# A scaled absolute value in the weights' conversion, a gap ahead of the gate tiles, ten sums on TensorE in place of twelve, and a new table of due times

## The chip, the cores and the metric

The kernel runs on one NeuronCore of a Trainium2 chip. The metric is the device time of one execution in microseconds (us). Before the change it is 534.67 us, the median of three runs (533.86 to 534.92). One further execution was taken with the profiler; everything that is said of single instructions comes from it.

## What is computed

Sliding-window attention over 8 batches, 8 heads, 576 positions of 64 elements, and behind it a feed-forward block with a gate:

```
scores = q @ k.T / 8, masked: heads 0-3 see the last 32 positions, heads 4-7 every 4th of the last 128
attn = softmax(scores); x = (attn @ v), heads side by side   # 8 x 576 x 512
h = relu(x @ w_in)                                           # 8 x 576 x 1024
conv = 3-tap convolution of h along the positions, per channel
out = (h * sigmoid(conv)) @ w_out                            # 8 x 576 x 512
```

The weights `w_in`, `w_out` and the taps arrive as 64-bit floats; everything else is 32-bit. The kernel reads each 64-bit weight as two 32-bit words and makes float32 numbers of them itself. Matrix products of `x` with `w_in` and of the gated `h` with `w_out` are made in a faster 32-bit format that keeps fewer bits, so each operand is kept as a high and a low part, and three products (high x high, high x low, low x high) are added.

## The kernel before

**Work.** The eight heads of a batch are handled in pairs, four pairs `p` a batch `b`, so 32 pairs; a pair is numbered `4 * b + p` here. Pairs with `p` 0 and 1 have the plain window (tensors `qk_p`, `v_p`), those with 2 and 3 the dilated one (`qk_d`, `v_d`). `attention` makes for each pair: two loads (L266 query and key, L268 value), the scores on TensorE (L294), a softmax on VectorE and ScalarE, a transpose on VectorE (L341), the product with the values on TensorE (L352), and the split of the result into a high part (`x..a`, ScalarE, L404) and a low part (`x..b`, VectorE, L407).

For the pairs in `EASED` the mask is added on TensorE (L281 puts it into the bank ahead of the scores), VectorE finds the maximum in the bank (L307, L309), and ScalarE makes nine exponentials with their sums (L318). For the others VectorE adds the mask (L323, L326), finds the maximum, subtracts it and sums (L328, L330, L334), and ScalarE makes one exponential of the whole tile (L332). Scores and products of the values stand in one set of banks, `att`, of which there is a single one: the scores of one pair, or the products of the values of one pair, hold it until the last reader is done. The scores of the pairs in `EARLY` stand in three other banks (`mm`, `mm`, `nn`).

`expert` makes for each batch the first product (L432: 16 groups of 12 matmuls with 288 columns, 1536 in all; even groups take columns 0 to 287 of `x`, odd groups 288 to 575), relu (L439), the taps (L450, L444), the sigmoid (L455), the gating (L457), the split into `g..a` and `g..b` (L460, L462), and the second product (L474: 24 matmuls with 512 columns for each 128 rows, 864 in all; `g` is the stationary operand, `wo` the one that moves). Results are copied out of the bank (L485) and stored (L488).

**Weights.** `weights` converts one block of 128 x 512 weights; there are 8 of `w_in`, 8 of `w_out`, and the small one of the taps. ScalarE takes the absolute value of the high words (L506); VectorE limits it from below (L508), shifts it (L510), puts sign and top bits back (L512), takes out the power of two (L515) and scales the low words (L517). For the blocks in `SUMMED` (counted 0 to 7 in `w_in`, 8 to 15 in `w_out`) ScalarE rounds to the high part (L523), TensorE sums the rest from three products (L526 to L528: with the identity, and twice with its negative), and ScalarE copies the low part out of the bank (L531). For the others VectorE adds (L533), ScalarE rounds (L538), VectorE subtracts (L539).

**Order.** No engine's order is written out. Each step is given to `Planner` with a cost, a due time, what it follows and which buffers it takes. The planner takes for each engine what can start first and, within `WINDOW`, what is due first. Due times come from the tables `DUE`, `PAIR`, `WI`, `WO`, `EXTRA`, and `SHIFT`, which moves single steps by their number. On the chip every engine works through its list strictly in that order. All transfers are issued from SyncE's list (SP), which waits in order too.

**Places.** The tiles of `const` lie one behind the other in each partition. By the program's addresses the tiles `wi` and `wo` begin 96 bytes past a multiple of 256 bytes, `x` and `g` 224 bytes past one; columns 288 on of `x` begin 96 bytes past one.

Of the kernel before, what the change touches and what calls it, by code (L numbers as in the profile page):

```python
# [8 lines left out]
F32 = mybir.dt.float32  # L9
# [4 lines left out]
AF = mybir.ActivationFunctionType  # L14
ALU = mybir.AluOpType
AX = mybir.AxisListType

B, H, S, D = 8, 8, 576, 64
# [18 lines left out]
    0: (983.85, 960.03, 1598.27, 67.97, 620.34, -923.1),  # L37
    1: (-938.0, 1528.76, 586.65, 116.27, 1083.92, -668.08),
    2: (652.26, -238.47, 216.19, -384.77, 936.91, 1546.14),
    3: (-577.95, 582.66, 797.36, 1055.27, 486.95, 100.42),  # L40
    4: (165.44, 367.0, 655.84, 266.33, 368.22, -114.96),
    5: (-900.42, 829.96, 667.81, -687.56, 659.06, -189.44),
    6: (8.73, -696.85, -879.8, 781.86, 1623.94, -212.82),
    7: (119.25, -702.72, 113.74, 318.1, 576.55, 91.32),
}
PAIR = {
    0: (-798.09, -868.3, -581.71, -552.22),
    1: (-227.57, -1850.41, -372.89, -477.4),
    2: (-1.4, 42.43, -131.58, 110.75),
    3: (118.94, 167.04, 351.66, 219.64),  # L50
    4: (363.37, 135.93, -216.08, 368.31),
    5: (629.07, 791.29, 654.94, 920.11),
    6: (1389.29, 1178.72, 41.99, 1049.45),
    7: (1485.93, 1267.62, 1424.81, 1415.74),
}
WI = (298.37, -257.47, 97.32, -1419.26, 580.38, -902.1, -1795.13, -709.05)
WO = (614.53, -200.78, 56.88, 710.98, 973.01, 906.23, 1376.69, 1432.54)
EXTRA = (-811.84, -256.46, -1474.23, 929.81, -481.76, 986.25, -195.54, -589.31, -887.09, -1471.19, -474.02, 685.32, 2263.81, 148.88, 1433.56, 2268.02, 97.62, -454.37, 119.84, 1449.84, 204.84, 29.37, 164.77, 787.77, 157.69, 1023.44, -135.34, -139.5, -1509.68, 1495.81, -788.12, -964.17, 519.88, -547.13, 138.9)

SHIFT = {  # L60
# [14 lines left out]
EASED = range(8)  # L75
EARLY = (1, 2, 3)
SUMMED = range(12)
# [21 lines left out]
class Planner:  # L99

    LATENCY = {"DVE": 0.05, "ACT": 0.05, "SP": 2.3, "POOL": 0.1, "E": 0.2, "S": 0.33, "T": 0.35, "V": 0.2}
# [5 lines left out]
              "TE": 0.11, "TV": 0.2, "TS": 0.2}  # L107
# [80 lines left out]
def attn_moe(ctx: ExitStack, tc: tile.TileContext, qk_p, qk_d, v_p, v_d, w_in, w_out, conv, mask, out):  # L188
    nc = tc.nc
# [25 lines left out]
    slots("x", NX, [128, S], F32R, 2)  # L215
    slots("g", NF, [128, S + REST], F32R, 2)
# [38 lines left out]
    def attention(b, p):  # L255
# [10 lines left out]
        lq = plan.add("SP", n * 0.00147, due - EXTRA[32], lambda: nc.sync.dma_start(  # L266
            out=qk.t[:, :n], in_=(qk_p, qk_d)[kind][b, p % 2]), uses=[qk])
        lv = plan.add("SP", 1.13, due - EXTRA[33], lambda: nc.sync.dma_start(  # L268
# [147 lines left out]
    def expert(b, ready, wired, wored, conved):  # L416
# [52 lines left out]
        for u, (first_col, rows) in enumerate(blocks):  # L469
# [7 lines left out]
            for k in range(NF):  # L477
                last = plan.add("PE", 0.68, out_due + by_block * u + by_step * k, lambda a=(first_col, ps, k): second(*a),
                                [last, wored[k], gates[k]], [ps, g[k]], "E")
                if b % 2 == 0:  # L480
                    read.setdefault((b, k), []).append(last)
# [10 lines left out]
    def weights(src, n, due, dst=None, pair=None, summed=False):  # L492
# [7 lines left out]
        last = plan.add("SP", 0.1 + 1.4 * f, due - EXTRA[34], lambda: nc.sync.dma_start(  # L500
            out=both(), in_=src.bitcast(I32).rearrange("p (n t) -> p n t", t=2)), uses=[raw])

        def step(cost, uses, run):
            return plan.add("DVE", 0.16 + cost * f, due + EXTRA[21], run, [last], uses)

        last = plan.add("ACT", 0.16 + 0.5 * f, due + EXTRA[20], lambda: nc.scalar.activation(  # L506
            out=words(u), in_=high().bitcast(F32), func=AF.Abs), [last], [raw, u])
        last = step(0.265, [u], lambda: nc.vector.tensor_scalar(  # L508
            out=words(u), in0=words(u), scalar1=2.0 ** -15, scalar2=None, op0=ALU.max))
        last = step(0.265, [u], lambda: nc.vector.tensor_scalar(  # L510
            out=ints(u), in0=ints(u), scalar1=3, scalar2=0x3fffffff, op0=ALU.logical_shift_left, op1=ALU.bitwise_and))
        last = step(0.53, [raw, u, t], lambda: nc.vector.scalar_tensor_tensor(  # L512
            out=ints(t), in0=high(), scalar=-0x40000000, in1=ints(u), op0=ALU.bitwise_and, op1=ALU.bitwise_or))
# [144 lines left out]
```

## Time and profile before

| | |
|---|---|
| time, median of 3 runs | 534.67 us (533.86 to 534.92) |
| the profiled execution's own time | 531.44 us |
| its span, first to last instruction | 529.7 us |
| mean granted TensorE clock | 0.993 |
| last matmul begins | 525.52 us after the span's start |

A row of the page's first part gives an engine's busy time, its share of the span and its instructions; the second part cuts the span in 40 slices of 13.2 us and gives a tenth-digit for each. A row of the timeline gives start and duration in us, engine, line and operation; a row of the windows gives, for a stretch, each engine's busy time and instructions, then TensorE's granted clock, the share of the DMA engines and GB/s. PE is TensorE, PEld its loads of the stationary operand, DVE VectorE, ACT ScalarE.

### The profile page before, as it was taken

The numbers are of one execution on the slowest core, as the hardware profiler recorded it, in microseconds if no ns is written. First come the engines' busy times: TensorE is split into PE (matmuls) and PEld (weight loads), VectorE is DVE, ScalarE is ACT, GpSimd is POOL, SyncE is SP. The second block draws the span as 40 slices with busy tenths as digits, with TensorE's granted clock in tenths as the row PEclk, the third lists the DMA queues.
The fourth block names the chain that finished last, engine by engine and source line by source line (L and its number), as shares of the span: only waits on it lengthen the run. The fifth ranks groups of instructions, "written<-read, shape, count | busy, mean of one in ns | idle before, by whom it ended". The sixth has DMA issues, their size and how long they took to land.

```text
span 529.7 us, 17200 instructions
## 1 busy us (share of the span) xinstructions
PE 507.5 (96%) x7668; PEld 440.5 (83%) x7668; DVE 396.1 (75%) x686; ACT 307.3 (58%) x661; POOL 1.4 (0%) x26
## 2 busy tenths in 40 slices
PE   4679999999999999999999999999999999999997
PEld 3458889898777799889999878998799978998885
DVE  5879999999987799888877887688556677475400
ACT  6776887756732279537776534666655534583410
POOL 1000000000000000000000000000000000000000
PEclk9979999999999999999999999999999999999999
DMA  8886663001344540250120444133211020010011
GB/s 296 312 292 221 186 208 111 1 1 41 111 160 150 179 153 0 75 187 2 29 73 1 152 145 131 51 101 104 79 42 41 0 88 24 1 41 22 31 49 59
DMA packets 17274, 52.33 MB, mean 99 GB/s; under 512 B 2096, under 2 KB 2480, under 8 KB 17200
## 3 DMA queue, kind: packets, MB, share of 16 engines
q1 hardware_dynamic: 17200, 51.23, 29.2%
q8 instruction: 60, 0.98, 0.8%
q14 instruction: 14, 0.11, 0.1%
HBM read 41.79 MB, written 9.44 MB: 97 GB/s over the span
## 4 chain that ended last, share of the span: by engine, by line
PE 93%; DVE 3%; issue 2%; ACT 1%; DMA 1%; SPq 0%; ACTq 0%; DVEq 0%
PE banks L474 39%; PE banks L432 39%; PE banks L352 7%; PE banks L294 6%; PE banks L526 1%; DMA qk<-in_qk_p_dram 1%; DVE s L339 1%; ACT s L318 1%; PE banks L281 0%; DVE m L307 0%; DVE r L517 0%; DVE pt L341 0%; DVE w L512 0%; PE banks L527 0%; PE banks L528 0%
## 5 line engine op out<-in xcount | busy, mean ns | idle before, releaser
L444 DVE SCALAR_TENSOR_TENSOR u<-u,conv_sb,u 128x576 f32<-128x576 f32 x128 | 104.2, 818 | 22.4 <-ACT u L450 20.6
L439 ACT ACTIVATE u<-banks 128x288 f32<-128x288 f32 x128 | 50.6, 410 | 50.9 <-PE banks L432 50.4
L457 DVE TENSOR_TENSOR u<-u,u 128x576 f32<-128x576 f32 x64 | 48.2, 758 | 22.7 <-ACT u L455 21.8
L455 ACT ACTIVATE u<-u 128x576 f32<-128x576 f32 x64 | 43.6, 686 | 31.0 <-DVE u L444 30.7
L485 ACT COPY u<-banks 128x512 f32<-128x512 f32 (+1 forms) x37 | 21.1, 574 | 61.4 <-PE banks L474 56.2
L432 PE MATMUL banks<-x5a,wi 128*128 128x288 f32 x192 | 53.5, 295 | 0.0
L450 ACT ACTIVATE u<-u,conv_sb 128x576 f32<-128x576 f32 x64 | 49.8, 778 | 1.5
L352 PEld LDWEIGHTS banks<-pt,v 32*64 32x64 f32 x2752 | 35.4, 133 | 15.8 <-issue 7.9
L294 PEld LDWEIGHTS banks<-qk 64*32 64x32 f32 x2432 | 30.0, 110 | 18.6 <-issue 9.7
L432 PE MATMUL banks<-x2a,wi 128*128 128x288 f32 x160 | 45.3, 298 | 0.0
L352 PE MATMUL banks<-pt,v 32*64 32x64 f32 (+2 forms) x2752 | 39.2, 229 | 6.2 <-issue 1.9
L294 PE MATMUL banks<-qk 64*32 64x64 f32 x2432 | 36.0, 234 | 9.3 <-DMA qk<-in_qk_p_dram 4.7
L432 PE MATMUL banks<-x0a,wi 128*128 128x288 f32 x160 | 44.9, 295 | 0.0
L432 PE MATMUL banks<-x6a,wi 128*128 128x288 f32 x160 | 44.7, 294 | 0.0
L432 PE MATMUL banks<-x4a,wi 128*128 128x288 f32 x160 | 44.5, 296 | 0.0
L432 PEld LDWEIGHTS banks<-x5a,wi 128*128 128x128 f32 x192 | 35.9, 187 | 0.4
L432 PEld LDWEIGHTS banks<-x6a,wi 128*128 128x128 f32 x160 | 30.0, 188 | 0.5
L432 PEld LDWEIGHTS banks<-x0a,wi 128*128 128x128 f32 x160 | 30.0, 188 | 0.4
L432 PEld LDWEIGHTS banks<-x2a,wi 128*128 128x128 f32 x160 | 30.0, 188 | 0.4
L432 PEld LDWEIGHTS banks<-x4a,wi 128*128 128x128 f32 x160 | 29.9, 188 | 0.2
L474 PE MATMUL banks<-wo,g4a 128*128 128x512 f32 x72 | 29.6, 413 | 0.0
L474 PE MATMUL banks<-wo,g1a 128*128 128x512 f32 x72 | 29.1, 406 | 0.0
(135 smaller groups left out, 1275.8 us busy)
## 6 DMA issues: line engine op xcount, KB each, us to landing
qk<-in_qk_d_dram SPq DMA_DIRECT2D x16, 672.0 KB, 4.9
qk<-in_qk_p_dram SPq DMA_DIRECT2D x16, 592.0 KB, 4.3
out_dram<-u SPq DMA_DIRECT2D x31, 256.0 KB, 2.0
v<-in_v_p_dram SPq DMA_DIRECT2D x16, 384.0 KB, 3.7
v<-in_v_d_dram SPq DMA_DIRECT2D x16, 384.0 KB, 3.5
raw<-in_w_in_dram SPq DMA_DIRECT2D x8, 512.0 KB, 5.4
raw<-in_w_out_dram SPq DMA_DIRECT2D x8, 512.0 KB, 4.1
out_dram<-u SPq DMA_DIRECT2D x10, 128.0 KB, 2.3
```

The lines of the kernel that those rows point to most:

```text
L294: nc.tensor.matmul(banks[quad * 32:quad * 32 + 32, at[bank], c * W:c * W + W], q, k, start=i == 0 and not eased, stop=i == len(parts) - 1, ...
L318: nc.scalar.activation(out=s.t[:, i, :], in_=banks[:, at[bank], c * W:c * W + W], func=AF.Exp, scale=SCALE, bias=m.t[:, i:i + 1], accum_ou ...
L339: last = plan.add("DVE", 0.755, step[5], lambda: nc.vector.tensor_tensor(out=nine(s.t), in0=nine(s.t), in1=wide(z.t), op=ALU.mult), [last] ...
L352: nc.tensor.matmul(banks[hd * 64:hd * 64 + 64, bank, o:o + n], v.t[quad * 32:quad * 32 + 32, block // 2, block % 2 * 64:block % 2 * 64 + 6 ...
L432: nc.tensor.matmul(bank(ps)[:, 0:HALF], wi[jw][fc][:, k * 128:k * 128 + 128], x[k].t[jx][:, hf * HALF:hf * HALF + HALF], start=(k == 0 and ...
L439: relu.append(plan.add("ACT", 0.4, due + 1.6 * u + relued, lambda fc=fc, hf=hf, ps=ps: nc.scalar.activation(out=h[fc].t[:, 1 + hf * HALF:1 ...
L444: nc.vector.scalar_tensor_tensor(out=body(c[fc]), in0=h[fc].t[:, k:S + k], scalar=conv_sb[:, k, fc:fc + 1], in1=body(c[fc]), op0=ALU.mult, ...
L450: t = plan.add("ACT", 0.777, d, lambda fc=fc: nc.scalar.activation(out=body(c[fc]), in_=body(h[fc]), func=AF.Copy, scale=conv_sb[:, 1, fc: ...
L455: t = plan.add("ACT", 0.686, d + shaped, lambda fc=fc: nc.scalar.activation(out=body(c[fc]), in_=body(c[fc]), func=AF.Sigmoid), [t], [c[fc ...
L457: t = plan.add("DVE", 0.755, d + times, lambda fc=fc: nc.vector.tensor_tensor(out=body(c[fc]), in0=body(c[fc]), in1=body(h[fc]), op=ALU.mu ...
L474: nc.tensor.matmul(bank(ps), g[k].t[jg][:, col:col + 128], wo[jw][k], start=(k == 0 and i == 0), stop=(k == NF - 1 and i == 2))
L485: t = plan.add("ACT", 0.16 + 0.00093 * (c1 - c0), out_due + by_block * u + copied, lambda ps=ps, o=o, c0=c0, c1=c1: nc.scalar.copy(out=chu ...
```

## The change

- ScalarE's absolute value of the high words gets a factor of 2^-112; VectorE's limit from below (L508) goes; the shift has no mask behind it any more, and only the sign is put back. One VectorE instruction fewer for each of the 17 conversions.
- A tile of 32 floats, `space`, lies between `x` and `g`: `g` and all that lies behind it move by 128 bytes, so that `g` begins 96 bytes past a multiple of 256 bytes, as `wo` does.
- `SUMMED` has ten blocks in place of twelve: of `w_in` 0 and 3 to 7, of `w_out` 0, 3, 4 and 6. Blocks 1 and 2 of both are now added on VectorE.
- `EASED` loses pair 5, `EARLY` becomes pairs 0, 1 and 3.
- The planner's costs of transfers, and of a change between attention and the second product (`"G"`), are others; all tables of due times are new. The program's lines lie 4 or 5 lower behind L216 (L474 becomes L478, L526 becomes L531).

```diff
-    0: (983.85, 960.03, 1598.27, 67.97, 620.34, -923.1),
+    0: (59.27, 488.41, 144.07, 13.74, 190.26, 24.51),
...
-EASED = range(8)
-EARLY = (1, 2, 3)
-SUMMED = range(12)
+EASED = (0, 1, 2, 3, 4, 6, 7)
+EARLY = (0, 1, 3)
+SUMMED = (0, 3, 4, 5, 6, 7, 8, 11, 12, 14)
...
-    LATENCY = {"DVE": 0.05, "ACT": 0.05, "SP": 2.3, "POOL": 0.1, "E": 0.2, "S": 0.33, "T": 0.35, "V": 0.2}
+    LATENCY = {"DVE": 0.05, "ACT": 0.05, "SP": 2.9, "POOL": 0.1, "E": 0.2, "G": 0.2, "S": 0.33, "T": 0.35, "V": 0.2}
...
-              "TE": 0.11, "TV": 0.2, "TS": 0.2}
+              "GV": 0.09, "GS": 0.09, "VG": 0.35, "SG": 0.35, "TE": 0.11, "TV": 0.2, "TS": 0.2}
...
     slots("x", NX, [128, S], F32R, 2)
+
+    const.tile([128, 32], F32, name="space")
     slots("g", NF, [128, S + REST], F32R, 2)
...
-                                [last, wored[k], gates[k]], [ps, g[k]], "E")
+                                [last, wored[k], gates[k]], [ps, g[k]], "G")
...
         last = plan.add("ACT", 0.16 + 0.5 * f, due + EXTRA[20], lambda: nc.scalar.activation(
-            out=words(u), in_=high().bitcast(F32), func=AF.Abs), [last], [raw, u])
+            out=words(u), in_=high().bitcast(F32), func=AF.Abs, scale=2.0 ** -112), [last], [raw, u])
         last = step(0.265, [u], lambda: nc.vector.tensor_scalar(
-            out=words(u), in0=words(u), scalar1=2.0 ** -15, scalar2=None, op0=ALU.max))
-        last = step(0.265, [u], lambda: nc.vector.tensor_scalar(
-            out=ints(u), in0=ints(u), scalar1=3, scalar2=0x3fffffff, op0=ALU.logical_shift_left, op1=ALU.bitwise_and))
+            out=ints(u), in0=ints(u), scalar1=3, scalar2=None, op0=ALU.logical_shift_left))
         last = step(0.53, [raw, u, t], lambda: nc.vector.scalar_tensor_tensor(
-            out=ints(t), in0=high(), scalar=-0x40000000, in1=ints(u), op0=ALU.bitwise_and, op1=ALU.bitwise_or))
+            out=ints(t), in0=high(), scalar=-0x80000000, in1=ints(u), op0=ALU.bitwise_and, op1=ALU.bitwise_or))
```

Two places show what the tables do. First SyncE's list, from its beginning: `qk` are queries and keys of a pair, `v` its values, `raw` the words of a block of weights. Before:

```order
L541 DMA kinds_sb_62<-in_mask_dram 128x320
L500 DMA raw0_155<-in_conv_dram 128x48
L266 DMA qk0_99<-in_qk_p_dram 128x1184
L500 DMA raw1_156<-in_w_in_dram 128x1024
L500 DMA raw2_157<-in_w_in_dram 128x1024
L266 DMA qk1_100<-in_qk_p_dram 128x1184
L266 DMA qk0_99<-in_qk_p_dram 128x1184
L268 DMA v0_101<-in_v_p_dram 128x768
```

After:

```order
L504 DMA raw0_156<-in_w_out_dram 128x1024
L504 DMA raw1_157<-in_conv_dram 128x48
L270 DMA qk0_99<-in_qk_p_dram 128x1184
L546 DMA kinds_sb_62<-in_mask_dram 128x320
L270 DMA qk1_100<-in_qk_d_dram 128x1344
L504 DMA raw2_158<-in_w_in_dram 128x1024
L272 DMA v0_101<-in_v_p_dram 128x768
L270 DMA qk0_99<-in_qk_d_dram 128x1344
L272 DMA v1_102<-in_v_d_dram 128x768
```

A block of `w_out` stands at the head of the list, where the masks stood, and dilated pairs come ahead of most plain ones.

Second ScalarE's list in the part that leads up to the first L432. `wi0` and `wo0` with a digit behind are the high parts of a block of `w_in` and `w_out` (`wi06` is block 6 of `w_in`), `wi1` and `wo1` the low parts, `x..a` the high parts of the pairs' results in their order, `x9` at the end of a row nine exponentials. Before, from the second set of exponentials on:

```order
L318 ACTIVATE s1_105,z1_111<-banks_164,m1_108 128x64 x9
L506 ACTIVATE w0_159<-raw3_158 128x512
L531 CAST wi16_81<-banks_164 128x512
L318 ACTIVATE s2_106,z2_112<-banks_164,m2_109 128x64 x9
L531 CAST wi13_78<-banks_164 128x512
L523 CAST wi05_72<-w1_160 128x512
L506 ACTIVATE w2_161<-raw0_155 128x512
L404 CAST x0a_115<-banks_164 128x2x128
L404 CAST x0a_115<-banks_164 128x2x160
L531 CAST wi15_80<-banks_164 128x512
```

After, from the second set on too:

```order
L322 ACTIVATE s2_106,z2_112<-banks_165,m2_109 128x64 x9
L322 ACTIVATE s1_105,z1_111<-banks_165,m0_107 128x64 x9
L408 CAST x0a_115<-banks_165 128x64
L408 CAST x0a_115<-banks_165 128x512
L513 ACTIVATE w1_161<-raw1_157 128x512
L528 CAST wo06_89<-w2_162 128x512
L528 CAST wo00_83<-w0_160 128x512
L536 CAST wo16_97<-banks_165 128x512
L513 ACTIVATE w2_162<-raw0_156 128x512
L408 CAST x1a_117<-banks_165 128x64
L408 CAST x1a_117<-banks_165 128x512
L322 ACTIVATE s2_106,z0_110<-banks_165,m1_108 128x64 x9
```

Two sets of exponentials now stand directly one behind the other ahead of the first `x0a`, and the blocks that are worked there belong to `w_out`, where they belonged to `w_in`.

More of the change, by code (lines that the diff above doesn't have):

```diff
@@ L36 @@
 DUE = {
-    0: (983.85, 960.03, 1598.27, 67.97, 620.34, -923.1),
[L38 to L44, printed above, removed]
+    0: (59.27, 488.41, 144.07, 13.74, 190.26, 24.51),
@@ L45 @@
+    1: (134.03, 1210.14, 1490.14, 168.23, 1457.54, 1223.28),
+    2: (361.13, 81.89, 1225.64, 427.18, 1708.88, -1503.02),
+    3: (403.31, 167.13, -307.1, 46.07, 42.34, -1116.84),
+    4: (1017.83, 1692.12, 2808.38, 3426.48, 267.18, -1219.05),
+    5: (1325.28, 211.45, 882.65, -806.86, 3587.67, 480.0),
+    6: (1758.91, 172.35, 422.21, -205.52, 55.09, -1548.12),
+    7: (314.85, -861.03, 288.71, 1692.96, 303.29, 36.77),
 }
 PAIR = {
-    0: (-798.09, -868.3, -581.71, -552.22),
-    1: (-227.57, -1850.41, -372.89, -477.4),
@@ L49 @@
[L49 to L54, printed above, removed]
-}
-WI = (298.37, -257.47, 97.32, -1419.26, 580.38, -902.1, -1795.13, -709.05)
-WO = (614.53, -200.78, 56.88, 710.98, 973.01, 906.23, 1376.69, 1432.54)
-EXTRA = (-811.84, -256.46, -1474.23, 929.81, -481.76, 986.25, -195.54, -589.31, -887.09, -1471.19, -474.02, 685.32, 2263.81, 148.88, 1433.56, 2268.02, 97.62, -454.37, 119.84, 1449.84, 204.84, 29.37, 164.77, 787.77, 157.69, 1023.44, -135.34, -139.5, -1509.68, 1495.81, -788.12, -964.17, 519.88, -547.13, 138.9)
@@ L60 @@
-SHIFT = {
[10 rows of a table removed]
+    0: (-866.06, -800.21, -1172.0, -1538.07),
+    1: (-308.05, -1636.99, -728.92, -865.51),
+    2: (-14.32, -211.48, -52.59, -7.44),
+    3: (2.55, 247.86, 28.54, 185.93),
+    4: (331.51, 106.82, 69.82, 348.9),
+    5: (764.07, 674.87, 845.97, 355.56),
+    6: (952.88, 578.25, 1186.65, 1151.92),
+    7: (1479.36, 1016.11, 1517.08, 1557.97),
+}
+WI = (-1606.48, 158.15, 516.12, 36.08, -73.43, 345.56, 530.68, 41.2)
+WO = (-626.55, 847.0, 1051.76, 180.42, -365.08, 1445.89, -712.69, 1516.06)
@@ L71 @@
+EXTRA = (150.65, -18.67, -1763.6, 354.89, 166.73, 459.81, 1116.51, -806.89, -1491.48, -1673.69, -1645.19,
+    -1786.5, 3435.95, -652.66, 608.62, -763.96, 188.52, -521.18, 559.1, 17.27, 452.19, 232.51, 182.64, -681.53,
+    301.97, 558.43, 504.78, 1103.29, 51.15, 911.07, -52.46, 1333.86, 1217.64, -73.41, 26.43)
+SHIFT = {
[10 rows of a table added]
 }
 MASKS = 70.0
-EASED = range(8)
-EARLY = (1, 2, 3)
-SUMMED = range(12)
+EASED = (0, 1, 2, 3, 4, 6, 7)
+EARLY = (0, 1, 3)
+SUMMED = (0, 3, 4, 5, 6, 7, 8, 11, 12, 14)
 LEFT = 16
@@ L265, in attention @@
         n = (S + KP, QD + KD)[kind]
-        lq = plan.add("SP", n * 0.00147, due - EXTRA[32], lambda: nc.sync.dma_start(
+        lq = plan.add("SP", n * 0.00131, due - EXTRA[32], lambda: nc.sync.dma_start(
             out=qk.t[:, :n], in_=(qk_p, qk_d)[kind][b, p % 2]), uses=[qk])
-        lv = plan.add("SP", 1.13, due - EXTRA[33], lambda: nc.sync.dma_start(
+        lv = plan.add("SP", 1.01, due - EXTRA[33], lambda: nc.sync.dma_start(
             out=v.t, in_=(v_p, v_d)[kind][b, p % 2]), uses=[v])
@@ L499, in weights @@
         ints = lambda b: b.t[:, :n].bitcast(I32)
-        last = plan.add("SP", 0.1 + 1.4 * f, due - EXTRA[34], lambda: nc.sync.dma_start(
+        last = plan.add("SP", 1.34 * f, due - EXTRA[34], lambda: nc.sync.dma_start(
             out=both(), in_=src.bitcast(I32).rearrange("p (n t) -> p n t", t=2)), uses=[raw])
```

20 rows, old and new, of the table SHIFT are left out of this document.

## The prediction

> **What bounds the kernel now.** First the page's head, busy times, slices and chain:
>
> ```profile
> span 529.7 us, 17200 instructions
> ...
> PE 507.5 (96%) x7668; PEld 440.5 (83%) x7668; DVE 396.1 (75%) x686; ACT 307.3 (58%) x661; POOL 1.4 (0%) x26
> ...
> PE   4679999999999999999999999999999999999997
> ...
> PE banks L474 39%; PE banks L432 39%; PE banks L352 7%; PE banks L294 6%; PE banks L526 1%; DMA qk<-in_qk_p_dram 1%; DVE s L339 1%; ACT s L318 1%; PE banks L281 0%; DVE m L307 0%; DVE r L517 0%; DVE pt L341 0%; DVE w L512 0%; PE banks L527 0%; PE banks L528 0%
> ```
>
> TensorE sets the end: it is busy 96% of the span and 93 in 100 of the chain are its own lines. What it does not work is 529.7 - 507.5 = 22.2 us. The windows say where:
>
> ```profile
> 0.00:10.00 10.00, 2.66 (x88) 1.93 (x94) 3.65 (x13) 5.92 (x17) 1.37 (x26) 1.00 0.77 277
> 10.00:20.00 10.00, 7.71 (x241) 5.20 (x241) 8.69 (x22) 9.43 (x54) 0.00 (x0) 1.00 0.84 291
> 20.00:30.00 10.00, 4.51 (x196) 3.35 (x204) 7.35 (x19) 5.67 (x21) 0.00 (x0) 0.86 0.98 373
> 30.00:40.00 10.00, 8.73 (x262) 6.61 (x253) 9.02 (x23) 8.02 (x45) 0.00 (x0) 0.80 0.77 258
> 40.00:50.00 10.00, 9.68 (x288) 8.22 (x287) 9.53 (x22) 6.33 (x20) 0.00 (x0) 1.00 0.59 197
> 150.00:200.00 50.00, 48.26 (x1079) 40.85 (x1078) 42.05 (x79) 20.99 (x40) 0.00 (x0) 1.00 0.48 157
> ```
>
> Up to 50 us TensorE works 2.66 + 7.71 + 4.51 + 8.73 + 9.68 = 33.29, so 16.7 us are lost at the start; 1.7 are lost between 150 and 200, the rest behind the last matmul. So the change is worth three things: what TensorE's own work shrinks by, what the start gains or loses, and waits that a new order brings later. An instruction saved on VectorE counts only in the start, since TensorE is never idle in the stretches behind it, the one between 150 and 200 apart.
>
> I work against the profiled execution: 531.44 us, its span of 529.7 and 1.74 around it. The median of the runs is 3.23 us above it; I add the difference to the median.
>
> **Two sums fewer.** One sum of a block of weights, inside the dense stream:
>
> ```profile
> 50.43 1.02 PE L526 MATMUL banks<-w,ident 128*128 128x512 f32 x2
> 50.89 0.80 PE L527 MATMUL banks<-r,minus 128*128 128x512 f32 x1
> 51.52 0.39 PE L528 MATMUL banks<-wi,minus 128*128 128x512 f32 x1
> 51.75 0.30 PE L432 MATMUL banks<-x1a,wi 128*128 128x288 f32 x1
> ```
>
> 51.75 - 50.43 = 1.32 us; twelve become ten: **-2.64 us**. VectorE takes an addition and a subtraction for each of the two blocks:
>
> ```profile
> L508 DVE TENSOR_SCALAR w<-w 128x512 f32<-128x512 f32 (+1 forms) x17 | 6.8, 398 | 4.4 <-ACT w L506 4.3
> L515 DVE TENSOR_SCALAR w<-w 128x512 int32<-128x512 int32 (+1 forms) x17 | 7.0, 410 | 0.3
> L512 DVE SCALAR_TENSOR_TENSOR w<-raw,w 128x512 int32<-128x512 int32 (+1 forms) x17 | 11.2, 662 | 0.6
> L539 DVE TENSOR_TENSOR wo<-w,wo 128x512 fp32r<-128x512 f32 x4 | 2.8, 688 | 0.0
> L533 DVE TENSOR_TENSOR w<-w,w 128x512 f32<-128x512 f32 x4 | 2.7, 686 | 0.0
> ```
>
> That is 2 x (0.69 + 0.69) = 2.8 us more, and the vanished limit saves 6.8 us (row L508). VectorE ends some 4 us lighter; TensorE hides this except in the start, where each block's chain is 0.4 us shorter. Should VectorE's cover be gone behind the start, the 4 us are an upper bound of what could come out. The factor on ScalarE I cost at nothing, since L506 stays one instruction.
>
> **One eased pair fewer.** Its mask on TensorE:
>
> ```profile
> 58.46 0.43 PE L281 MATMUL banks<-kinds_sb,ones 128*128 128x64 bf16 x5
> 58.82 1.13 PE L294 MATMUL banks<-qk 64*32 64x64 f32 x80
> ```
>
> 58.82 - 58.46 = **-0.36 us**. The pair costs VectorE more and ScalarE less; that is in the start's walk below.
>
> **The place of g.** While a matmul runs, the next one's stationary operand is loaded. For the second product the load (`g`, 224 past a multiple of 256) is 128 bytes off the moving operand (`wo`, 96) before, and even with it after. The trace has both cases in the first product: even groups move `x` from 224, odd ones from 96, beside `wi` at 96. Three groups follow one another, each beginning with this row:
>
> ```profile
> 248.09 0.29 PE L432 MATMUL banks<-x2a,wi 128*128 128x288 f32 x1
> ...
> 249.69 0.29 PE L432 MATMUL banks<-x2a,wi 128*128 128x288 f32 x1
> ...
> 251.27 0.30 PE L432 MATMUL banks<-x2a,wi 128*128 128x288 f32 x1
> ```
>
> The even group takes 1.60 us for 12 matmuls, the odd one 1.58, so 1.6 ns a matmul less where the places agree. The second product:
>
> ```profile
> 521.32 0.39 PE L474 MATMUL banks<-wo,g0a 128*128 128x512 f32 x1
> ...
> 525.52 0.40 PE L474 MATMUL banks<-wo,g7a 128*128 128x512 f32 x1
> ```
>
> 18 steps in 4.20 us: 233 ns each. 864 of them at 1.6 ns less give -1.4 us; if the gain grows with the columns (512 against 288), 2.8 ns and -2.5. One row stands against it: the last L474 ahead of an L432 has the next load (`wi`, 96) even with `wo` already:
>
> ```profile
> 469.20 0.40 PE L474 MATMUL banks<-wo,g7a 128*128 128x512 f32 x1
> 469.43 0.29 PE L432 MATMUL banks<-x2a,wi 128*128 128x288 f32 x1
> ```
>
> It steps in 230 ns, as far as a row shows no less than the 233 of the others (there are 30 such steps in the trace, this is the last). If it speaks for all, the even and odd groups differ by the moving operand's own place, and g's place gains nothing. And the shortest step in the trace is
>
> ```profile
> 220.40 0.39 PE L474 MATMUL banks<-wo,g6b 128*128 128x512 f32 x1
> 220.62 0.40 PE L474 MATMUL banks<-wo,g6a 128*128 128x512 f32 x1
> ```
>
> 0.22 us (224 ns): all steps at that would give -7.5 us. A loss is bounded by the same 2.5 us above nothing, if the first product's difference comes from the other cause and turns round. Range -7.5 to +2.5; I take **-1.9**, between -1.4 and -2.5, the nearest rows.
> The Trainium skill ("SBUF — State Buffer", section on the two separate sides) speaks against this edit: by it TensorE's port never waits on anyone, contention being a matter of the port that VectorE and GpSimd share. By that the term is 0 and the forecast would be some 1.9 us higher; the 1.6 ns between even and odd groups do not fit that rule, the step at 469.20 does.
>
> **The start.** Here I walk along the new order with durations of the old trace. In the old start the DMA engines were full:
>
> ```profile
> 6.00:8.00 2.00, 1.89 (x76) 1.39 (x76) 0.64 (x2) 0.73 (x2) 0.00 (x0) 1.00 1.03 420
> ```
>
> so 0.4 MB a us, and the second load of the list was in at 4.06:
>
> ```profile
> 4.06 0.22 ACT L506 ACTIVATE w<-raw 128x24 f32<-128x24 f32 x1 [1.53 <-DMA raw<-in_conv_dram]
> ```
>
> Ahead of and with pair 2's queries the new list has 0.52 (`w_out`) + 0.02 + 0.61 + 0.08 + 0.69 + 0.52 + 0.39 + 0.69 = 3.5 MB; with the first 0.5 MB in by then, they land at 11.6 and the scores end at 12.9. VectorE meanwhile works block 4 of `w_out`, mask and maximum of pair 5 (no longer eased, so on VectorE), the maximum of pair 3, the sums of pair 5, block 0 of `w_in` (two steps like L515, two like L512, 2.2 us) and pair 3's normalization; it reaches pair 2's maximum at 16.2 and ends it at 18.1. Nine exponentials step as here:
>
> ```profile
> 13.52 0.31 ACT L318 ACTIVATE s<-banks,m 128x64 f32<-128x64 f32 x1 [0.46 <-DVE m L311]
> ...
> 16.14 0.70 ACT L506 ACTIVATE w<-raw 128x512 f32<-128x512 f32 x1
> ```
>
> 2.6 us, so pair 2 leaves the single attention bank at 20.8, and only then the first values can run in it. Before, the values ran at
>
> ```profile
> 20.26 1.12 PE L352 MATMUL banks<-pt,v 32*64 32x32 f32 x84 [0.70 <-ACT s L318]
> ...
> 24.57 0.89 PE L352 MATMUL banks<-pt,v 32*64 32x32 f32 x68 [1.68 <-DVE z L338]
> ...
> 29.65 1.60 PE L352 MATMUL banks<-pt,v 32*64 32x32 f32 x84 [1.66 <-DVE x1b L407]
> ...
> 39.21 0.29 PE L432 MATMUL banks<-x1a,wi 128*128 128x288 f32 x1
> ```
>
> Each turn of the bank needs ScalarE's split and VectorE's subtraction, and these stand behind blocks of weights and exponentials in their lists: (29.65 - 20.26) / 2 = 4.7 us a turn. My walk gives the new turns at 20.9, 26.8, 33.0, 36.2 and 39.2, 4.6 a turn. But now five values stand ahead of the dense stream, not three; with one more sum (block 3 of `w_in`, whose part on VectorE ends at 41.0) it begins at 42.2. Until there TensorE has done five sets of scores (1.2 each), four masks (0.36), five values (1.2), five sums (1.32) and six L432 (1.2 with their entries): 21.3 us, 20.9 lost. In the old start the scores and values took longer than that, as here and in the row at 29.65:
>
> ```profile
> 5.93 1.36 PE L294 MATMUL banks<-qk 64*32 64x64 f32 x72 [2.71 <-DMA qk<-in_qk_p_dram]
> ```
>
> With 1.36 for the scores and 1.4 for the values 1.8 us fewer are lost, 19.1. I take 19.7, between the two and nearer to these rows: **+3.0 us** against 16.7. Bounds: the walk misses by a turn of 4.7 either way, -1.7 to +7.7.
>
> **Later waits** I take as before (1.7 us between 150 and 200): the runs of attention in the dense stream are as many (25 and 27 before, 26 and 27 after), so their entries cost the same. Bounds: -1.7 to +4.
>
> **Sum:** -2.64 - 0.36 - 1.9 + 3.0 = -1.9 us: profiled 529.5, median 534.67 - 1.9 = **532.8 us**.
>
> **Rivals.**
> - *The place gives nothing* (the even step at 469.20): -2.64 - 0.36 + 3.0 = 0, 534.7 us.
> - *The place gives much*, 5 to 7.5 us (224 ns is reached in the trace, and the longer matmul has more to lose): 534.67 - 0 - 6.2 = 528.5 us.
> - *The start comes a turn sooner*, because VectorE saves 0.4 us in every block of the start and no later wait takes it back: -1.7 in place of +3.0, 528.1 us.
> - *Slower: weights of the wrong matrix first.* Blocks 4, 6 and 0 of `w_out` are worked before the stream begins, which needs `w_in`: 3 x 2.2 = 6.6 us of VectorE's time in front of the first product. It decides once VectorE cannot give a block of `w_in` in the time in which TensorE uses one up: 24 matmuls of 0.133, 3.2 us, against 2.2 plus whatever softmax stands between. Then up to 6.6 us more are lost: 534.67 - 1.9 + 6.6 = 539.4 us. Against it: three blocks and four pairs of batch 0 are ready at 42.
> - *The slow clock hits the stream.* After TensorE's sparse stretch the clock was halved:
>
> ```profile
> 28.00:30.00 2.00, 0.35 (x24) 0.35 (x32) 1.22 (x4) 1.96 (x12) 0.00 (x0) 0.50 0.97 354
> ```
>
> In my walk the sparse stretch is 28 to 36; a halved window of the same 6.8 us would reach into the stream and cost up to 3.4: 536.2 us.
>
> **How the numbers follow.** Two runs of this kernel cannot be told apart below 0.2%, 1.1 us. Forecast 33% (in its spread 24 faster, 7 same, 2 slower), nothing from the place 20% (7, 9, 4), much from the place 15% (all faster), early start 12% (11 faster, 1 same), wrong weights first 13% (all slower), slow clock 7% (1, 2, 4). Together faster 58, same 19, slower 23. The range, 526.5 to 538, leaves out the place's full 7.5 us with an early start, and the upper part of the wrong weights.
>
> **What would show it.** Ten L531 groups of sums with 1.3 us each; steps of L478 at 231 ns (230.5 where the place gives 1.9, 233 where nothing, 227 and less where much); first values near 20.9, first dense L436 near 42 and 19 to 20 us lost up to 50; no wait above 1.5 us behind 50. Wrong if TensorE idles behind 50 for blocks of `w_in`, if the first values run before 18, or if the sum of TensorE's busy time falls by much more than 5 us.

## The result, and the profile after

| | before | after |
|---|---|---|
| time, median | 534.71 us (4 runs, 533.86 to 534.92) | 528.64 us (4 runs, 527.55 to 529.17) |
| the profiled execution's own time | 531.44 us | 529.17 us |
| its span | 529.7 us | 527.4 us |

The ratio is 0.9887 (95% interval 0.9866 to 0.9907): 6.1 us faster. The forecast was 532.8 us, with a range of 526.5 to 538.

The page's head, busy times, TensorE's slices and the chain, after:

```profile
span 527.4 us, 17134 instructions
...
PE 505.9 (96%) x7656; PEld 442.2 (84%) x7656; DVE 393.4 (75%) x675; ACT 304.9 (58%) x642; POOL 1.4 (0%) x26
...
PE   4579999999999999999999999999999999999997
...
PE banks L436 40%; PE banks L478 38%; PE banks L356 7%; PE banks L298 6%; PE banks L531 2%; ACT s L322 1%; DMA raw<-in_w_out_dram 1%; DMA qk<-in_qk_d_dram 1%; PE banks L533 0%; PE banks L532 0%; PE banks L285 0%; DVE x2b L411 0%; SPq L504 0%; SPq L270 0%; DVE w L517 0%
```

The bound is the same: TensorE, busy 96% of the span. The windows after (columns as before: the engines' busy time and instructions, TensorE's granted clock, DMA share, GB/s):

```profile
0.00:10.00 10.00, 2.87 (x143) 2.42 (x144) 4.17 (x12) 5.08 (x11) 1.37 (x26) 1.00 0.79 284
10.00:20.00 10.00, 7.43 (x205) 4.48 (x187) 8.71 (x21) 6.64 (x27) 0.00 (x0) 1.00 0.95 346
20.00:30.00 10.00, 6.14 (x167) 4.05 (x168) 9.32 (x23) 7.33 (x40) 0.00 (x0) 0.65 0.90 326
30.00:40.00 10.00, 8.34 (x264) 5.71 (x263) 6.94 (x16) 7.06 (x28) 0.00 (x0) 0.67 0.63 207
40.00:50.00 10.00, 10.00 (x197) 7.13 (x196) 7.83 (x17) 5.56 (x17) 0.00 (x0) 0.83 0.59 208
```

TensorE works 34.8 of the first 50 us, so 15.2 are lost, against 16.7 before and 19.7 forecast. But it works more slowly there: its clock is down to 0.65 and 0.67 between 20 and 40 us (0.86 and 0.80 before), so less idle time does not mean a shorter start. TensorE's timeline of after in the start (start, duration, operation, in brackets the idle time ahead and what ended it):

```profile
20.95 0.33 PE L356 MATMUL banks<-pt,v 32*64 32x64 f32 x4 [2.71 <-ACT s L322]
...
30.82 1.87 PE L356 MATMUL banks<-pt,v 32*64 32x64 f32 x88
...
35.48 1.44 PE L356 MATMUL banks<-pt,v 32*64 32x32 f32 x84
...
38.58 1.12 PE L356 MATMUL banks<-pt,v 32*64 32x32 f32 x84 [1.66 <-DVE x2b L411]
...
42.04 0.45 PE L436 MATMUL banks<-x2a,wi 128*128 128x288 f32 x1
...
42.90 1.27 PE L356 MATMUL banks<-pt,v 32*64 32x32 f32 x84
```

The first values run at 20.95 (the walk gave 20.9; four matmuls there, the other 84 from 22.43), the first product begins at 42.04 (42.2). The values between them do not stand where the walk has them: they run at 30.82, 35.48 and 38.58 in place of 26.8, 33.0 and 36.2, and the fifth, at 39.2 in the walk, at 42.90, behind the beginning of the first product. The second product, 18 steps of one row group in the timeline of after:

```profile
519.17 0.39 PE L478 MATMUL banks<-wo,g4a 128*128 128x512 f32 x1
...
523.25 0.39 PE L478 MATMUL banks<-wo,g1a 128*128 128x512 f32 x1
```

4.08 us, 227 ns each; before it was 4.20 and 233. Over all steps that follow one another directly the means are 232.7 ns before (732 steps) and 227.7 after (782). Last, TensorE's waits between 50 and 500 us, the one row of before and then the two of after (the total in us, how often, the longest; "issue" is a wait that no event of the profile explains):

```profile
PE banks L294 <- issue: 1.7, 2, 1.3
```

```profile
PE banks L356 <- issue: 1.7, 2, 1.1
PE banks L298 <- issue: 0.8, 1, 0.8
```

### The profile page after: what moved, and what is told of

It is laid out like the page before. It is cut to its first block, busy times and chain, and to the rows that moved or that the text cites. A ratio compares the mean times of both kernels' runs of the same rounds, so it can differ in the third digit from the quotient of the medians.

```text
span 527.4 us, 17134 instructions
## 1 busy us (share of the span) xinstructions
PE 505.9 (96%) x7656; PEld 442.2 (84%) x7656; DVE 393.4 (75%) x675; ACT 304.9 (58%) x642; POOL 1.4 (0%) x26
## 4 chain that ended last, share of the span: by engine, by line
PE 92%; DMA 3%; ACT 2%; issue 1%; DVE 1%; SPq 0%; ACTq 0%
PE banks L436 40%; PE banks L478 38%; PE banks L356 7%; PE banks L298 6%; PE banks L531 2%; ACT s L322 1%; DMA raw<-in_w_out_dram 1%; DMA qk<-in_qk_d_dram 1%; PE banks L533 0%; PE banks L532 0%; PE banks L285 0%; DVE x2b L411 0%; SPq L504 0%; SPq L270 0%; DVE w L517 0%
## 5 line engine op out<-in xcount | busy, mean ns | idle before, releaser
L356 PEld LDWEIGHTS banks<-pt,v 32*64 32x64 f32 x2752 | 36.4, 137 | 16.7 <-issue 7.3
L356 PE MATMUL banks<-pt,v 32*64 32x64 f32 (+2 forms) x2752 | 40.5, 233 | 7.2 <-ACT s L322 3.9
L436 PE MATMUL banks<-x3a,wi 128*128 128x288 f32 x160 | 45.7, 302 | 0.0
L436 PE MATMUL banks<-x1a,wi 128*128 128x288 f32 x160 | 45.2, 298 | 0.0
L298 PEld LDWEIGHTS banks<-qk 64*32 64x32 f32 x2432 | 29.8, 109 | 16.7 <-DMA qk<-in_qk_p_dram 6.9
L436 PE MATMUL banks<-x5a,wi 128*128 128x288 f32 x128 | 36.2, 299 | 0.0
L436 PEld LDWEIGHTS banks<-x3a,wi 128*128 128x128 f32 x160 | 29.9, 188 | 1.0 <-ACT u L443 0.2
L436 PEld LDWEIGHTS banks<-x1a,wi 128*128 128x128 f32 x160 | 30.0, 188 | 0.4
L478 PE MATMUL banks<-wo,g1a 128*128 128x512 f32 x72 | 28.7, 398 | 0.0
```

The costliest lines, as they stand in the source:

```text
L298: nc.tensor.matmul(banks[quad * 32:quad * 32 + 32, at[bank], c * W:c * W + W], q, k, start=i == 0 and not eased, stop=i == len(parts) - 1, ...
L356: nc.tensor.matmul(banks[hd * 64:hd * 64 + 64, bank, o:o + n], v.t[quad * 32:quad * 32 + 32, block // 2, block % 2 * 64:block % 2 * 64 + 6 ...
L436: nc.tensor.matmul(bank(ps)[:, 0:HALF], wi[jw][fc][:, k * 128:k * 128 + 128], x[k].t[jx][:, hf * HALF:hf * HALF + HALF], start=(k == 0 and ...
L478: nc.tensor.matmul(bank(ps), g[k].t[jg][:, col:col + 128], wo[jw][k], start=(k == 0 and i == 0), stop=(k == NF - 1 and i == 2))
```

## The experiments

In what follows "before" is always the kernel before as run beside the experiment (medians of 534.04 to 534.26 over 9 to 29 runs).

### The place of g: moved alone, taken back alone

In the old order only `g` is moved:

```diff
     slots("x", NX, [128, S], F32R, 2)
+    const.tile([128, 32], F32, name="space")
     slots("g", NF, [128, S + REST], F32R, 2)
```

> The kernel before with one edit: the 128-byte gap ahead of g, nothing else; every engine's order is the old one. Theory A (the place of g against wo sets the second product's step): the step falls from 232.7 to 227.7 ns, as in the changed kernel, and the time falls by 864 x 5.0 ns = 4.3 us, ratio about 0.992. Rival B (the steps are shorter because of the new order, or of fewer other reads at the same time): the step stays at 232.7 and the time within 0.2%. Rival C (nothing ever waits there): the same as B.

Measured: 530.94 us (528.35 to 531.78) against 534.04, ratio 0.9935 (0.991 to 0.9961). In the changed kernel the tile `space` is put behind `g`, so that only `g` goes back and what lies behind it stays moved:

```diff
-    const.tile([128, 32], F32, name="space")
     slots("g", NF, [128, S + REST], F32R, 2)
+    const.tile([128, 32], F32, name="space")
```

> The changed kernel with the gap behind g in place of ahead of it: g is 128 bytes off wo again, the tiles behind g stay where the change put them. Theory A: steps of 232.7 ns and 4.3 us above the changed kernel, so about 1.7 us below the kernel before (ratio 0.997). Rival B (the order): steps of 227.7 and the changed kernel's time, ratio 0.989. Rival D (not g but the tiles behind it, which moved too): as B.

Measured: 533.63 us (531.84 to 535.44), ratio 0.999 (0.997 to 1.001), so 5.0 more than the changed kernel. Eighteen steps of the second product, first with `g` moved in the old order, then with `g` moved back in the new one:

```profile
520.86 0.39 PE L475 MATMUL banks<-wo,g0a 128*128 128x512 f32 x1
...
524.94 0.39 PE L475 MATMUL banks<-wo,g7a 128*128 128x512 f32 x1
```

```profile
523.66 0.39 PE L478 MATMUL banks<-wo,g4a 128*128 128x512 f32 x1
...
527.87 0.40 PE L478 MATMUL banks<-wo,g1a 128*128 128x512 f32 x1
```

4.08 us and 4.21 us. Over all steps that follow one another the means are 228.6 ns (732 steps) with `g` moved in the old order and 233.0 (782) with `g` moved back in the new one: 4.1 and 5.2 ns a step, which in 864 steps are 3.5 and 4.5 us. The step follows `g`'s place in both orders; the tiles behind `g` have no part in it. This edit alone is worth 3.1 to 5.0 us by the runs.

### Which place: 224 for all, and 64 bytes off

`wi`, `wo` and `g` all 224 bytes past a multiple of 256, in the old order (a tile of 32 floats ahead of `wi`, another ahead of `x`):

> The kernel before with two gaps of 128 bytes, ahead of wi and ahead of x: wi and wo begin 224 past a multiple of 256, as g does; x stays at 224 and 96 for even and odd groups. If it is the distance between the two operands that counts: second product's step 227.7 ns; in the first product the even groups (now 0 apart) take 131.7 and the odd ones (now 128 apart) 133.5, exchanged against before. If it is each operand's own place: the step stays at 232.7 (g is where it was) or moves with wo, and even and odd groups stay at 133.5 and 131.7. Time by the first: -4.3 us.

Measured: 531.17 us (527.7 to 531.57), ratio 0.994 (0.9914 to 0.9966), and 228.6 ns a step of the second product. What tells the theories apart is the first product. Three groups in a row begin here; by their number the first and third are odd (`x` at 96, `wi` now at 224), the second is even (both at 224):

```profile
246.02 0.29 PE L434 MATMUL banks<-x5a,wi 128*128 128x288 f32 x1
...
247.62 0.29 PE L434 MATMUL banks<-x5a,wi 128*128 128x288 f32 x1
...
249.20 0.30 PE L434 MATMUL banks<-x5a,wi 128*128 128x288 f32 x1
```

The odd group takes 1.60 us, the even one 1.58 (133.4 and 131.7 ns a step over all groups of 12 that stand undivided). Before it was the other way round (131.8 and 133.4). It is the distance between the stationary and the moving operand that counts, not the place of either. Next `g` at 160, 64 bytes past `wo`, in the new order (`space` of 48 floats in place of 32):

> The changed kernel with a gap of 192 bytes in place of 128: g begins 64 bytes past wo's place, 160 past a multiple of 256. If only equal places are quick: a step near 232.7 ns and 4.3 us above the changed kernel. If any distance but 128 is quick: 227.7 and the changed kernel's time. If the step grows with the distance, half way: about 230 ns, +2 us.

Measured: 533.58 us (531.5 to 537.69), ratio 0.9984 (0.9959 to 1.001), 233.3 ns a step (781 steps; one more, of 427 ns, is left out): as slow as 128 bytes off. Of the three distances tried only 0 is quick.

Two stationary operands could matter: a step's own, and the next one's, which is loaded while the step runs. In the middle of a product both have the same place; where one product follows the other they differ. The steps of the second product ahead of one of the first have `wi` as their next operand, which is even with `wo` with or without the change. With `g` off they take 232.5 ns (30 steps, before) and 231.7 (19, `g` moved back in the new order), with `g` even 229.9 (30, `g` moved in the old order) and 229.8 (19, the changed kernel). The steps of the first product ahead of one of the second have `g` as their next operand. Those of the odd groups, even in themselves, take 131.1 ns where `g` is off (53 steps in the three profiles with `g` at 224) and 131.5 where it is even (179 in nine profiles with `g` at 96). So the quick step goes with the place of the step's own stationary operand, and the next one's place shows no effect. Why the place matters at all stays open.

### The words, in the new order and in the old

The new order with the old words: limit and shift as one step of the planner, so that the order stays.

```diff
-            out=words(u), in_=high().bitcast(F32), func=AF.Abs, scale=2.0 ** -112), [last], [raw, u])
+            out=words(u), in_=high().bitcast(F32), func=AF.Abs), [last], [raw, u])
+        def limited():
+            nc.vector.tensor_scalar(out=words(u), in0=words(u), scalar1=2.0 ** -15, scalar2=None, op0=ALU.max)
+            nc.vector.tensor_scalar(out=ints(u), in0=ints(u), scalar1=3, scalar2=0x3fffffff,
+                                    op0=ALU.logical_shift_left, op1=ALU.bitwise_and)
```

> The changed kernel, its order and places, but the words made as before: no factor on ScalarE, and the limit from below back on VectorE as an instruction of its own ahead of each shift (17 more). Theory A (VectorE hides it once TensorE's stream is dense; in the start six blocks lie ahead of the stream on a VectorE that is busy four fifths): +0.4 us for each of some three to six blocks, 1 to 2.5 us above the changed kernel, ratio to before about 0.993. Rival B (VectorE has slack in the start as well): within 0.5 us of the changed kernel. Rival C (all 17 on the path): +7 us.

Measured: 532.11 us (530.71 to 532.71), ratio 0.9961 (0.9947 to 0.9976): 3.5 us more than the changed kernel, more than I expected. And the old order with the new words, the limit's step issuing nothing:

> The kernel before, its order and places, with the words made as in the change: the limit's step stays in the planner's list but issues nothing. Theory A (VectorE's saving counts only in the start): 1 to 2 us below the kernel before, ratio 0.996 to 0.998. Rival B: nothing. Rival C: -7 us.

Measured: 533.92 us (532.92 to 534.77), ratio 1.0 (0.9986 to 1.0014). A miss: in the old order the same saving is worth nothing. Where it goes in the new one is taken up in the last experiment.

### Every sum twice

Each of the ten sums is issued twice in the new order (`add()` two times):

> The changed kernel with each of its ten sums issued twice on TensorE (the second overwrites the first with the same result). If a sum costs its 1.32 us wherever the stream is dense and is partly hidden in the start: four to five of them in the start, so 7 to 13 us above the changed kernel, and each of the later ones 1.32 us: it shows what taking two away was worth, 2.6 us. If sums fall into waits: below 4 us.

Measured: 535.61 us (533.82 to 538.64), ratio 1.0037 (1.0016 to 1.0059), 7.0 more than the changed kernel. One of the doubled sums in the stream:

```profile
46.58 1.02 PE L531 MATMUL banks<-w,ident 128*128 128x512 f32 x2
47.03 0.80 PE L532 MATMUL banks<-r,minus 128*128 128x512 f32 x1
47.67 0.39 PE L533 MATMUL banks<-wi,minus 128*128 128x512 f32 x1
47.90 1.02 PE L531 MATMUL banks<-w,ident 128*128 128x512 f32 x2
```

The repetition begins 1.32 us after the sum. Five of the ten stand in the stream (44.60 to 71.95 in the changed kernel's timeline): 5 x 1.32 = 6.6 of the 7.0. The five of the start put the first product off from 42.0 to 44.5; in this profile 2.1 of these 2.5 us are regained further on. Before, five of twelve stood in the start too (15.32 to 37.88). So the two that went are, by their number, two of the stream.

### TensorE kept occupied in the start

The slow clock between 20 and 40 us follows a stretch in which TensorE has little to do. Here it gets something: matmuls of the ones by themselves, 30 ahead of the first scores, 12 and 8 ahead of the first and fourth values.

```diff
+        def fill(n):
+            for _ in range(n):
+                nc.tensor.matmul(banks[:, 3, 384:512], ones, ones, **ONE)
...
             at = held()
+            fill(30 if NP * b + p == 5 else 0)
...
+            fill({3: 12, 5: 8}.get(NP * b + p, 0))
             begun = set()
```

> The changed kernel with 50 idle products of ones with ones into columns of a bank that nothing reads: 30 ahead of the first scores, 12 ahead of the first values, 8 ahead of the fourth. They only fill TensorE's waits. Theory A (the start loses time because the clock is halved after idle stretches: 13.7 us of halved clock between 23 and 37): the clock stays whole through the start and the time falls by 1 to 3 us, with less spread from run to run. Rival B (VectorE and ScalarE set the start, TensorE's clock does not matter): same time. Rival C (the fill delays the scores): up to 2 us more.

Measured: 524.75 us (524.41 to 527.05), ratio 0.9841 (0.982 to 0.9862), 3.9 less than the changed kernel. Then the 30 alone:

> The changed kernel with only the first of the three fills: 30 matmuls of the ones by themselves (128x128, into columns that nothing reads) ahead of the first scores; the 12 and 8 ahead of the first and fourth values are left out. Question: which part of the 3.9 us between 528.64 and 524.75 comes from the first 10 us, where the clock no longer starts at half, and which from keeping TensorE occupied later. Theory A, the beginning alone: the scores and sums up to 12.7 us run at full clock, VectorE's chain starts earlier, and most of the gain is there: 525 to 526.3, first product near 40.5. Theory B, the later stretch: the clock is halved again from 23 to 36 us as in the changed kernel, so that only some 1 us is kept: 527.2 to 528.2.

Measured: 524.81 us (523.81 to 526.18), ratio 0.9825 (0.9792 to 0.9858): the first fill does it all. The windows of the changed kernel, and then of this one:

```profile
8.00:10.00 2.00, 1.78 (x85) 1.33 (x74) 1.20 (x3) 1.80 (x6) 0.00 (x0) 1.00 0.93 339
...
23.00:37.00 14.00, 12.15 (x306) 7.69 (x300) 11.43 (x25) 8.88 (x42) 0.00 (x0) 0.52 0.73 243
```

```profile
8.00:10.00 2.00, 1.33 (x76) 1.16 (x77) 1.30 (x3) 1.70 (x5) 0.00 (x0) 0.72 1.03 417
10.00:13.00 3.00, 3.00 (x34) 1.55 (x22) 2.93 (x8) 2.25 (x9) 0.00 (x0) 0.62 1.03 411
...
23.00:37.00 14.00, 10.55 (x356) 7.06 (x349) 12.78 (x28) 10.98 (x46) 0.00 (x0) 0.74 0.83 292
```

Of theory A's numbers the first product came (40.13 against some 40.5) and the time nearly (524.81, where its range begins at 525). Its mechanism came in part only. The first scores do run faster (0.97 us for the 72 matmuls at 6.96, against 1.36 at 6.91 without the fill), but the first sum does not, and the first values run at 20.89, no sooner than before. The first sum, from its beginning to the row behind it, in the changed kernel and then in this one:

```profile
10.62 2.07 PE L531 MATMUL banks<-w,ident 128*128 128x512 f32 x2
...
13.04 0.43 PE L285 MATMUL banks<-kinds_sb,ones 128*128 128x64 bf16 x5
```

```profile
10.48 2.01 PE L538 MATMUL banks<-w,ident 128*128 128x512 f32 x2
...
12.79 0.43 PE L291 MATMUL banks<-kinds_sb,ones 128*128 128x64 bf16 x5
```

2.42 us and 2.31 us, where a sum in the stream takes 1.32. So the clock is slow there in both, and the 1.00 in the changed kernel's row for 8 to 10 us is no measurement: the clock records of its profile begin at 12.7 us. What differs is the stretch from 23 to 37 us, at 0.52 without the fill: about half of it is back at full speed (0.74), and the first product comes 1.9 us sooner. And the "issue" waits behind 50 us, 2.5 us after, are gone in this run: between 50 and 500 no wait of TensorE is left in that view. With three fills 1.0 us of them is left. Why they go is open. More of the same, 32 ahead of pair 2's scores as well and 24 ahead of the fourth values:

> The filled kernel with more of the same: 32 matmuls of the ones ahead of pair 2's scores as well (2.64 us of waiting for its queries there) and 24 in place of 8 ahead of the fourth values (2.15 us of waiting for VectorE). If the halved clock of 13.3 to 16.7 and of 37.2 to 40.6 is what these idle stretches cost, the clock stays whole around them: the sums of 15.2 to 17.4 and 37.1 to 39.8 take 2.2 in place of some 2.4 and 2.7 us, and 523.7 to 524.5 comes out beside 524.75. If what is late there is VectorE's or the transfers' work anyway, it stays at 524.5 to 525.2; the additional fill delays the real work, if the queries or the transposed blocks come before it ends, by up to 1 us.

Measured: 526.06 us (524.48 to 527.8), ratio 0.9842 (0.981 to 0.9873), no better, and the timeline shows the price that was expected:

```profile
35.84 2.72 PE L278 MATMUL banks<-ones 128*128 128x128 bf16 x24 [1.66 <-DVE x2b L418]
...
41.82 0.29 PE L443 MATMUL banks<-x2a,wi 128*128 128x288 f32 x1
```

At half clock 24 of them take 2.72 us, longer than the wait; the first product begins at 41.82 in place of 40.13. And the old order, with `g` moved and its own idle stretches filled:

> The kernel before with g moved to w_out's place, as in the first experiment, and with fills in its own idle stretches: 30 matmuls of the ones ahead of the first scores, 30 ahead of the second pair's (3.42 us idle there) and 16 ahead of the third values (1.86). Question: is filling worth as much in the old order, and does the changed kernel keep an advantage by its order and words once both starts are filled. If the halved clock costs the old order's start what it costs the new one's: 527 to 528 beside 530.94, with the first product near 40; the rest of the change (two sums and an eased pair, words) is then the 2 to 3.5 us down to 524.75. If the old order's start waits for transfers and VectorE whatever the clock: 530 to 531.

Measured: 527.12 us (526.5 to 528.71), ratio 0.9866 (0.9834 to 0.9899), 3.8 less than without the fills. So filling is worth the same in both orders (30 matmuls in the new one, 76 in three places in the old one), and what the changed kernel has over the old one with `g` moved is the same with it (527.12 - 524.81 = 2.3) and without (530.94 - 528.64 = 2.3). These 2.3 us are no more than the sums and the eased pair come to by the prediction's terms (2.64 + 0.36), so order and words together bring nothing beyond them.

### The words once more, with the start filled

> The kernel with the one fill ahead of the first scores (524.81), with the old words of the weights again (the limit on VectorE and the shift in one step, no factor on ScalarE), as in the fifth experiment, where they cost 3.5 us in the changed kernel. Question: does the words' saving count because VectorE's chain sets the start, or because the longer chain happened to draw a halved clock into more of it. Theory A, VectorE's chain: the three blocks of weights worked ahead of the first values and the two behind take 0.4 us each again whatever the clock, so that 2 to 3.5 us are lost here too: 526.8 to 528.3. Theory B, the clock: with the beginning at full clock the words are worth their 0.4 us in one or two blocks only: 525.0 to 525.8.

Measured: 527.58 us (526.99 to 528.43), ratio 0.988 (0.9864 to 0.9897): 2.8 more than with the new words, theory A's size. Its place is another. The first product begins at 39.87 here, no later than the 40.13 with the new words. TensorE's waits between 50 and 500 us in this run, then two windows of this run and two of the same kernel with the new words:

```profile
PE banks L363 <- issue: 0.6, 2, 0.3
PE banks L363 <- DVE x5b L418: 0.6, 1, 0.6
PE banks L304 <- issue: 0.5, 1, 0.5
PE banks L443 <- ACT u L450: 0.4, 1, 0.4
PE banks L304 <- ACT s L328: 0.3, 1, 0.3
```

```profile
50.00:70.00 20.00, 19.44 (x425) 17.32 (x422) 19.22 (x39) 14.58 (x44) 0.00 (x0) 1.00 0.55 172
70.00:90.00 20.00, 19.45 (x410) 17.48 (x409) 19.03 (x36) 17.87 (x46) 0.00 (x0) 1.00 0.59 193
```

```profile
50.00:70.00 20.00, 20.00 (x417) 17.72 (x397) 19.12 (x38) 15.54 (x52) 0.00 (x0) 1.00 0.58 189
70.00:90.00 20.00, 20.00 (x420) 18.57 (x419) 19.02 (x34) 17.85 (x41) 0.00 (x0) 1.00 0.55 176
```

VectorE is busy 19 of 20 us in both. With the old words TensorE loses 1.1 us in these 40; with the new ones nothing. The waits that name VectorE or ScalarE behind it (`x5b`, `u`, `s`) are there only with the old words. Both runs have the same granted clock between 20 and 44 us, 0.79. So with the start filled the saving is paid out in the stream, where VectorE has next to no reserve, not in the start. Without the fill it is less clear: the profile of the new order with the old words has three waits for VectorE and ScalarE too (`x5b`, `u` and `s`, 1.7 us together), which the changed kernel's does not have, but its first product also begins later, at 43.51 against 42.04, though its clock between 20 and 44 us is not lower (0.71 against 0.64). One profile each cannot divide the 3.5 us between the two.

## Why the forecast came out as it did

- **What bounds the kernel** was right: TensorE's own work, its start, and little else.
- **Two sums fewer, -2.64.** Right for TensorE. 1.32 us a sum in the stream was measured by repeating it, and by their number both that went stood there. What their additions on VectorE cost, and what the eased pair is worth, no run separates.
- **The place of g, -1.9.** Right that the distance between `g` and `wo` sets the step, and too small. By the steps 864 x 5.0 ns = 4.3 us; by the runs 3.1 (moved alone) and 5.0 (taken back). The term failed where I scaled from the first product by columns: 1.6 ns at 288 columns became 2.8 at 512, and 5.0 were there. It also named the wrong load: not the next one's but the step's own operand counts. The row that I held against the term, the step of 230 ns at 469.20, misled for the same reason: there the next operand was even and the step's own was not. It was a quick one by chance; the 30 such steps take 232.5 on average, hardly less than the 232.7 of the others. The rival "the place gives much", at 5 to 7.5, was nearer in its time (528.5 us), but that is luck: it takes 6.2 for the place, more than any run shows, and with it the +3.0 of the start, which did not come. The Trainium skill ("SBUF — State Buffer", the section on the two separate sides), as the prediction reads it, gives 0 for this term; the first four runs decide against that 0 here.
- **The start, +3.0.** Both ends of the walk came (20.95 and 42.04 against 20.9 and 42.2), the turns between them did not (up to 4.0 us off, and four values ahead of the first product, not five), so that the end came so near is in part luck. And the comparison was wrong. I set it against the profiled execution of before, whose first product began at 39.21, and added the 3.23 us between that execution and the median as if they were spread evenly. They were not. The first product of the old order in two other profiles, with the new words (534.74 us) and with `g` moved (530.85 us):

```profile
42.62 0.29 PE L432 MATMUL banks<-x1a,wi 128*128 128x288 f32 x1
```

```profile
43.22 0.29 PE L433 MATMUL banks<-x1a,wi 128*128 128x288 f32 x1
```

What sets these executions apart is the clock. Here are the granted clock between 20 and 44 us and the beginning of the first product in the profiles without a fill (that of the doubled sums left out):

| | granted clock, 20 to 44 us | first product |
|---|---|---|
| before | 0.86 | 39.21 |
| old order, new words | 0.72 | 42.62 |
| old order, `g` moved | 0.69 | 43.22 |
| old order, all at 224 | 0.64 | 43.60 |
| new order, `g` moved back | 0.72 | 40.72 |
| after | 0.64 | 42.04 |
| new order, `g` 64 bytes off | 0.59 | 43.44 |
| new order, old words | 0.71 | 43.51 |

In each order, the last row apart, the first product comes the later, the lower the clock is. The profiled execution of before had less of the halved clock than the others, and at a like clock (0.72, 0.64) the new order's first product is 1.6 to 1.9 us sooner, not 3.0 later. That is the size of the rival "the start comes a turn sooner" (-1.7), and the last row, late at 0.71, speaks for its reason, VectorE's saving; but that is one profile each, and the fifth values now follow behind the first product. In medians I take the term as about 0. This and the place are the 4.2 us between 532.8 and 528.64: 3.0 here, and 1.2 to 3.1 there; what that is more than 4.2, up to 1.9, the new order costs, as the next point shows.
- **An instruction saved on VectorE counts only in the start.** This step failed. In the old order the saving brings nothing at all (sixth run). In the new one it is worth 3.5 us, and 2.8 with the start filled, where it comes out behind the first product. The 4 us that I named as the upper bound "should VectorE's cover be gone" are the right size only by luck: they are 6.8 saved less 2.8 added, and these runs put back the 6.8 alone, of which about half came out. The new order itself costs about as much as the words bring back, as a sum shows. Place -4.3, sums -2.6 and the eased pair -0.4 make -7.3; the new order with the old words is 2.0 below before, so the order by itself costs 5.3 by this sum, and with the new words 1.2 (with 3.1 for the place, as in the first experiment, 4.1 and nothing).
- **Later waits, 0.** 2.5 us after against 1.7 before. Other profiles make the difference larger: between 50 and 500 us TensorE is idle for 4.2 and 3.7 us in the new order with `g` off, and for 1.0 to 1.7 in the old order with `g` moved, with all at 224 and with the new words. So a part of what the new order costs may lie here; it stays within the bound of +4.
- **The slow clock hits the stream.** It came (0.83 in the window from 40 to 50) and costs the start more than the stream; by the filled start 3.9 us hang on the start together with the waits that go with it. Wrong weights first did not come: no wait for a block of `w_in` shows in the waits after.

## What to carry to other kernels

Where the bound engine's step is a few hundred nanoseconds and repeats some hundred times, compare the addresses of its two operands modulo 256 bytes before anything else: a tile of 128 bytes was worth more here (3.1 to 5.0 us) than two removed sums (2.6). Don't carry the difference between a profiled execution and the median as a constant: find the stage in which it lies, and compare with more than one profile of the kernel before, with the granted clock of each beside it. And before a saving on a second engine is put down as hidden, ask whether the same edit takes that engine's reserve away: here it was busy 19 of 20 us between 50 and 90 us, and the saving paid in the new order alone, where it made good about what that order costs.

## What the runs showed of the hardware

- In a row of matmuls in the 32-bit format of fewer bits, each with a stationary operand of its own, the step of 512 columns is 227.7 to 228.6 ns where its stationary and its moving operand lie at the same place modulo 256 bytes, and 232.7 to 233.3 where they are 64 or 128 bytes apart; with 288 columns 131.7 to 131.9 against 133.3 to 133.4. The place of the next stationary operand, loaded meanwhile, shows no effect (131.1 ns with it off, 131.5 with it even).
- Thirty matmuls without use at the very beginning made the changed kernel 3.8 us faster, with the granted clock from 23 to 37 us at 0.74 in place of 0.52; in the old order 76 in three places did the same. That the clock is the way by which they work fits the profiles, but no run holds the clock and changes the rest. Twenty more, filled in later, added nothing, and 24 at half clock cost 2.72 us.
- The versions with the first fill (524.81 us) and with three fills (524.75) are the quickest and can't be told apart; the first is 9.3 us under the kernel before.
